# A planned attention and feed-forward kernel: 1 KB rings, a third q buffer, the sums' addition set back, the last matrix in token buffers, last units 256 and 192, two chunks not gated

## The chip, the cores and the metric

One core of one Trainium2 chip runs the whole program. The metric is the device time of one execution in microseconds; a time is the median of several runs. The engines are named as the profile names them: PE is TensorE (PEld its weight loads), DVE is VectorE, ACT is ScalarE, POOL is GpSimd, SP is SyncE, which issues all DMAs here.

## What is computed

Attention over 4 batches, 8 heads, 576 positions and 64 columns per head, in which each row keeps its 32 largest scores; then two feed-forward layers over the 2304 tokens (d_model 512). All inputs and the output are float32.

```python
scores = scale * np.matmul(q, k.transpose(0, 1, 3, 2))
kth = np.partition(scores, -top_k, axis=-1)[..., -top_k:-top_k + 1]   # top_k = 32
scores = np.where(scores >= kth, scores, -1000000000.0)
attn = np.exp(scores - np.max(scores, axis=-1, keepdims=True))
attn = attn / (np.sum(attn, axis=-1, keepdims=True) + 1e-09)
x = np.matmul(attn, v)                       # then heads side by side: 2304 x 512
h = x @ w_in;  x = np.maximum(0.01 * h, h) @ w_out            # d_ff = 2048
x = np.maximum(np.maximum(x @ w1, x @ w2), x @ w3) @ w_out2   # d_ff = 768
```

## The kernel before

**Arithmetic.** The weights arrive as pairs of 32-bit words (float64). DVE puts each 512 columns together in three passes (lines 498, 501, 504); ACT and POOL scale them and split them into two float16 parts, high and low (`split3`, lines 355 to 357). Every float32 product is three float16 matmuls (`three`, lines 874 to 876: high x high, high x low, low x high).

**Attention.** It goes in 72 steps. A step is one block of 128 tokens for one pair of heads, or a block of 64 tokens for two pairs; a batch has 18 steps. PE multiplies q and k into the one PSUM buffer `s` (line 716), ACT copies the scores to `S` (721, three buffers). DVE finds the 32 largest of each row in four MAX8 and three MATCH_REPLACE8 per half step (736, 738) and makes the mask (791, 795). ACT takes the exponential (786); ACT and POOL split it into `phl` (800, 802), and SP transposes it into `pt` by a DMA (805). PE multiplies by v into the one PSUM buffer `av` (831 to 833, the tile `sav` in the profile). DVE adds a small constant to the row sums (838) and inverts them (840), ACT scales the result into `xs` (842), ACT and POOL split it into `xhl`, and after the last pair of heads of a block SP transposes it into the token tile `xu` of its unit (868).

**Feed-forward units.** `ffn(u)` handles 192, 128, six times 256, 192 and 256 tokens. Phase H/Y makes 16 H tiles (`h_tile`, 12 matmuls each, evicted by ACT at 918 into a float tile) and adds each into four accumulators (`y_acc`). Then the result is scaled and split into `yh`, `yl` (968 to 973), with a norm over it (980). Phase M/O makes 6 tiles, each of three products joined by maximum (`m_tile`, 1011 and 1015), and adds them up (`o_acc`); ACT evicts the result (1043) and SP stores it (1053). `hilo` splits a float tile at 925 and 931. The batch's blocks finish in the order of `ORDER`; the last batch ends with two blocks of 128 and 64 tokens after 2112.

**Weights.** `prep_w` prepares w_in (kind i, 8 chunks), w_out (o, 8), w1 to w3 (t, 6) and the last matrix (z, 4). H of unit 0 waits for w_out, H of unit 1 for the last matrix, and M of unit 0 for all of t and z. The last matrix is loaded into the ring `raw`, which q, k and v of the later batches use too; its loads are put behind the loads of q and k of the second batch, and those of later batches behind it. A chunk with a gate is not loaded before a given store of the first split q or k.

**Order.** `Plan.op` registers each operation with its engine, a planned duration, what it reads and writes, and a priority. `Plan.run` (lines 125 ff.) then plays the program through with these durations: of the operations that can start at about the same time on an engine it takes the one with the lowest priority value, and an operation that needs a new buffer waits for one. The resulting order of starts is the order of each engine's queue on the chip; waits for data are made from the data flow. Tile rings have the sizes of `NB`. A ring in the set handed to `Plan` hands out buffers in any order, another in the order of the program. Second names (`hH`, `kM`, ...) limit how many buffers of a ring a phase holds: H tiles, M tiles, W for weights.

Of the kernel before, what the change touches and what calls it, by code (L numbers as in the profile page):

```python
# [27 lines left out]
PS = 2048.0  # L28
LNPS = float(np.log(PS))
P = 128  # L30
# [5 lines left out]
UN = 256  # L36
VC = 11
F0, F1, F2, F3, HB = (0, P), (P, P), (2 * P, P), (3 * P, P), (4 * P, 64)
ORDER = [[F0, HB, F1, F2, F3], [F0, F1, F2, F3, HB], [HB, F0, F1, F2, F3], [F0, F1, F2, F3, HB]]
UNITS = [192, 128] + [256] * 6 + [192, 256]  # L40

# [26 lines left out]
class Node:  # L68
    __slots__ = ("eng", "dur", "fn", "pr", "succ", "nd", "ready", "bufs", "eps", "idx", "dma")


class Plan:
# [12 lines left out]

    def op(self, eng, dur, fn, r=(), w=(), pr=0.0, dma=0.0):
        n = Node()
        n.eng, n.dur, n.fn, n.pr, n.dma = eng, dur, fn, pr, dma
        n.succ, n.ready, n.idx, n.eps = [], 0.0, len(self.nodes), self.eps
# [27 lines left out]
    eps = EPS  # L117
# [5 lines left out]
    def run(self):  # L123
# [10 lines left out]
        while len(order) < total:  # L134
# [46 lines left out]
            for m in n.succ:  # L181
                m.nd -= 1
                m.ready = max(m.ready, end + self.LAT.get((n.eng, m.eng), 0.2))
                if m.nd == 0:
                    pend[m.eng].append(m)
# [34 lines left out]
def attention_moe_kernel(ctx, tc, qk, v, w_in, w_out, w123, w2o, outT):  # L220
# [8 lines left out]

    NB = {"xu": 2, "raw": 2, "hl": 1, "k2": 7, "kt": 4, "qt": 2, "vt": 4, "S": 3, "w": 1, "m": 2, "nb": 2, "pp": 1,  # L230
          "phl": 1, "pt": 1, "r": 2, "xs": 1, "xhl": 1, "f16t": 4, "yj": 1,
          "s": 1, "av": 1, "acc": 2, "h": 4, "junk": 1, "xcap": 2, "pr": 8, "ph": 4, "ra": 3, "fi": 6, "ft": 9, "rw": 3, "fz": 3, "rc": 2, "hH": 3, "hM": 3, "hW": 1, "kH": 2, "kM": 5, "fH": 2, "fM": 2}
    PSUM_TAGS = ("s", "av", "acc", "h")
    plan = Plan(NB, {"raw", "av", "junk", "hl", "k2", "h", "f16t", "rc"})
    op = plan.op
# [16 lines left out]
    def fbuf(tag, ph, shape, dt=F32):  # L252
        b = buf(tag, shape, dt)
        b.also = (plan.buf({"h": "h", "k2": "k", "f16t": "f"}[tag] + ph, lambda: 1),)
        return b
# [103 lines left out]
    KT, QT, VT, ES = {}, {}, {}, {}  # L359
    ZL = [(("w", "z", 3), "ld")]  # L360

# [99 lines left out]

    SC = {}
    CVK = "iotz"
    CW = 512
    CVX = 0.06
    PRW0 = -13.5
    GATES = {1: [("d", 0, 0, 0, 1)], 2: [("d", 0, 1, 0, 1)]}

    def prep_w(kind, c, parts, hi, lo, colnorm, n2c, s, bi, pr, tags, guard=((), (), []), gate=()):
# [8 lines left out]
        for i, saps in enumerate(parts):  # L478
            nf = sum(n for _, n in saps)
            f = buf(tags[1], [P, 768 if tags[1] == "raw" else 512], I32)  # L480
            o = 0
            for sap, n in saps:
                raw = buf(tags[0], [P, 768])
                op(SP, 0.55, lambda raw=raw, sap=sap, n=n: Y.dma_start(raw().bitcast(I64)[:, :n], sap),
                   w=[raw, (key, "ld")] + ([(f, "ld")] if tags[1] in ("raw", "k2") or tags[0] == "raw" else []),
                   r=list(gate) + zr + (zf + [("l1", hp, a) for hp in range(HP) for a in range(2)] * (kind == "z") + guard[2] * (tags[1] == "raw") if kind in "tz" else []), pr=PRW0 if (kind, c) == ("i", 0) else pr,
                   dma=dma(P * n * 8))
# [64 lines left out]
    def wkeys(kind, cs):  # L552
        return [("W", kind, c, x, i) for c in cs for x in range(2) for i in range(WK[kind][1])]
# [6 lines left out]
    def c1(t, c):  # L560
        return t[:, c:c + 1]
# [27 lines left out]
    def w2_prep(e, pr):  # L589
        for hp in range(HP):  # L590
            if (1, hp) not in seen:
                seen.add((1, hp))
                prep_batch(1, hp)
        prep_w("z", e, [[(w2o[e, i], 384) for i in range(2)]], [w2[:, e, 0]], [w2[:, e, 1]],
               None, c1(cz, e), c1(sz, e), c1(bz, e), pr, ("raw", "fz" if e < 3 else "raw"),
               ({0: ["ZB"], 3: [("ZZ", 2)]}.get(e, []), [("ZZ", e - 1)] if e in (1, 2) else [],
                [("ZZ", e - 1)] if e else ["ZB"]))
# [79 lines left out]

    EXPP = 4
    COLD = 1.7
    NCOLD = 8  # L680
# [13 lines left out]
    def attention(i):  # L694
# [143 lines left out]
        op(DVE, 0.07, lambda: V.tensor_scalar(r()[:n, 0:nh].rearrange("p (x h) -> p x h", h=2),  # L838
                                             av()[:n, 0:nh // 2, :, 64], 1e-9 * PS, None, op0=ALU.add), r=[avb], w=[(r, 0)], pr=pr)
        op(DVE, 0.08, lambda: V.reciprocal(r()[:n, 4:4 + nh], r()[:n, 0:nh]), r=[(r, 0)], w=[(r, 1)], pr=pr)  # L840
# [45 lines left out]

    MAXP = 40
    FINP = 40
    CS = 0.8
# [3 lines left out]
    def ffn(u, pr0, between=None):  # L893
# [4 lines left out]
        t3 = 3 * mm(N)  # L898
        acc, ak, ast, a0 = accs(N)
        clock = [pr0]  # L900
# [7 lines left out]
        def h_tile(f):  # L908
            pr = tick(1.3)
            c = f // (FCI // P)  # L910
            p = fbuf("h", "H", [P, 512])
            wk = wkeys("i", [c]) + wkeys("o", range(8)) * (u == 0) + wkeys("z", range(4)) * (u == 1)
            for k in range(KC):
                op(PE, t3, lambda k=k: three(p()[:, :N], lambda x: wi[:, x, k, f * P:(f + 1) * P],
                                             lambda x: xu()[:, x, k, :N], k == 0, k == KC - 1),
                   r=xk + wk, w=[p], pr=pr)
            rr = fbuf("k2", "H", [P, 2, UN])
            op(ACT, act(N, True, 1), lambda: A.activation(rr()[:, 0, :N], p()[:, :N], AF.Prelu,  # L918
# [81 lines left out]
        def m_tile(f):  # L1000
            t = fbuf("k2", "M", [P, 2, UN])
            wk = wkeys("t", [f]) + (wkeys("t", range(NF2)) + wkeys("z", range(4))) * (u == 0)
# [185 lines left out]
```

## Time and profile before

| | |
|---|---|
| median of 3 runs | 1149.49 us (1147.88 to 1154.09) |
| profiled execution | 1152.11 us |
| its span, first to last instruction | 1150.2 us |
| PE / PE weight loads busy | 912.4 / 797.7 us |
| DVE busy | 973.6 us |
| ACT / POOL busy | 757.3 / 680.6 us |
| DMA moved | 125.79 MB, 44.6% of 16 engines' span |

The profile comes from one execution. An engine is busy while one of its instructions runs; what it waited for before an instruction is read from the semaphore that came last. L838 is line 838 of the kernel. A row of waits gives who waited, for whom, total us, times, and the longest. In the timeline a merged row gives its start, its length, engine, line, operation, tiles written and read, shapes and count.

### The profile page before, as it was taken

Reading aid. Unit: us, or ns where it says so; the run is one execution under the profiler, and the core shown is the slowest. Engines: PE = TensorE matmul, PEld = TensorE weight load, DVE = VectorE, ACT = ScalarE, POOL = GpSimd, SP = SyncE. Lnnn points to the kernel's source line nnn. Section 1 sums busy time; section 2 is a strip of 40 time slices with the busy share of each in tenths; the row PEclk is TensorE's granted clock in tenths of the full one; section 3 lists DMA queues with packets and bytes.
Section 4 is the critical chain, followed back from the end, with each engine's and each line's share of the span. In section 5 each row is a group of like instructions: output and inputs, shape, how many; then the busy total and the mean of one; then the engine's idle time right before and its main releaser. Section 6 shows DMA issues by size and latency. Waiting matters only on the chain.

```text
span 1150.2 us, 27408 instructions
## 1 busy us (share of the span) xinstructions
PE 912.4 (79%) x10294; PEld 797.7 (69%) x10294; DVE 973.6 (85%) x2154; ACT 757.3 (66%) x1625; POOL 680.6 (59%) x1054
## 2 busy tenths in 40 slices
PE   3253246853299799999899989989998998998998
PEld 2131235742199788887688778878887887898987
DVE  3989999989989999999899899899999999995001
ACT  7667747886457767567778665686786666665331
POOL 5555646875446766566777655575787556555231
PEclk9999998975599999999999999999999999999999
DMA  7758455654354423235574333364573433332000
GB/s 234 250 141 264 147 159 166 176 122 134 96 122 88 96 64 83 62 73 131 139 184 118 65 79 70 60 149 78 146 164 66 87 77 52 79 64 52 20 1 19
DMA packets 268549, 125.79 MB, mean 109 GB/s; under 512 B 237440, under 2 KB 255360, under 8 KB 266368
## 3 DMA queue, kind: packets, MB, share of 16 engines
q1 hardware_dynamic: 268416, 124.04, 44.6%
q8 instruction: 81, 1.33, 0.5%
q14 instruction: 52, 0.43, 0.1%
HBM read 62.65 MB, written 14.16 MB: 67 GB/s over the span
## 4 chain that ended last, share of the span: by engine, by line
PE 40%; DMA 14%; DVE 11%; POOL 7%; ACT 6%; issue 5%; SPq 1%; POOLq 0%; ACTq 0%; DVEq 0%
DMA pt<-phl 12%; PE h L874 7%; PE h L875 7%; PE h L876 7%; PE acc L875 4%; DVE m L736 4%; PE acc L874 4%; PE acc L876 4%; DVE w L738 3%; PE sav L716 3%; POOL phl L802 3%; PE sav L831 2%; PE sav L832 2%; PE sav L833 2%; POOL f16t L931 1%
## 5 line engine op out<-in xcount | busy, mean ns | idle before, releaser
L736 DVE MAX8 m<-w 128x8 f32<-128x576 f32 x432 | 309.7, 746 | 0.1
L931 POOL TENSOR_TENSOR f16t<-k,f16t 128x256 f16<-128x256 f32 (+2 forms) x220 | 142.8, 651 | 195.1 <-ACT f16t L925 184.1
L738 DVE MATCH_REPLACE8 w<-m,w 128x576 f32<-128x576 f32 x288 | 211.9, 741 | 0.0
L802 POOL TENSOR_TENSOR phl<-pp,phl 128x576 f16<-128x576 f32 x144 | 183.7, 1281 | 45.5 <-ACT phl L800 43.9
L874 PE MATMUL h<-k,w 128*128 128x256 f16 (+2 forms) x720 | 187.0, 264 | 7.8 <-ACT k L971 5.5
L875 PE MATMUL h<-k,w 128*128 128x256 f16 (+2 forms) x720 | 186.9, 264 | 3.7 <-POOL k L973 3.6
L876 PE MATMUL h<-k,w 128*128 128x256 f16 (+2 forms) x720 | 186.8, 264 | 0.0
L716 PE MATMUL sav<-kt,qt 128*128 128x288 f16 (+5 forms) x800 | 110.1, 288 | 77.1 <-ACT S L721 56.2
L875 PE MATMUL acc<-f16t,wo 128*128 128x256 f16 (+2 forms) x640 | 164.9, 262 | 4.7 <-POOL f16t L931 4.6
L874 PE MATMUL acc<-f16t,wo 128*128 128x256 f16 (+2 forms) x640 | 165.0, 262 | 0.0
L876 PE MATMUL acc<-f16t,wo 128*128 128x256 f16 (+2 forms) x640 | 165.0, 262 | 0.0
L874 PE MATMUL h<-xu,wi 128*128 128x256 f16 (+1 forms) x576 | 155.8, 270 | 5.0 <-ACT k L918 2.2
L876 PE MATMUL h<-xu,wi 128*128 128x256 f16 (+1 forms) x576 | 155.8, 271 | 0.0
L875 PE MATMUL h<-xu,wi 128*128 128x256 f16 (+1 forms) x576 | 155.8, 271 | 0.0
L800 ACT ACTIVATE phl<-pp 128x576 f16<-128x576 f32 x144 | 97.8, 681 | 65.0 <-DMA pt<-phl 27.8
L786 ACT ACTIVATE pp<-S,nb,colt 128x576 f32<-128x576 f32 x144 | 121.5, 860 | 20.6 <-POOL nb L776 12.7
L716 PEld LDWEIGHTS <-qt 128*128 128x128 f16 (+1 forms) x800 | 65.2, 109 | 99.8 <-issue 75.9
L798 POOL TENSOR_TENSOR pp<-pp,S 128x576 f32<-128x576 f32 x72 | 92.2, 1280 | 69.8 <-DVE S L795 42.9
L925 ACT ACTIVATE f16t<-k 128x256 f16<-128x256 f32 (+2 forms) x220 | 85.3, 392 | 59.9 <-DVE k L1015 57.2
L831 PE MATMUL sav<-vt,pt 128*128 128x65 f16 (+1 forms) x800 | 91.2, 202 | 38.5 <-DMA pt<-phl 34.1
L918 ACT ACTIVATE k<-h,colt 128x256 f32<-128x256 f32 (+2 forms) x160 | 71.1, 451 | 70.5 <-PE h L876 69.3
L721 ACT ACTIVATE S<-sav 128x576 f32<-128x576 f32 x144 | 92.8, 644 | 32.2 <-PE sav L716 18.4
(133 smaller groups left out, 2629.5 us busy)
## 6 DMA issues: line engine op xcount, KB each, us to landing
w<-in_w SPq DMA_DIRECT2D x18, 512.0 KB, 3.9
w<-in_w_in SPq DMA_DIRECT2D x8, 1024.0 KB, 6.6
w<-in_w_out SPq DMA_DIRECT2D x8, 1024.0 KB, 4.9
raw<-in_qk SPq DMA_DIRECT2D x24, 288.0 KB, 3.4
dqk<-hl SPq DMA_DIRECT2D x48, 144.0 KB, 2.5
kt<-dqk SPq DMA_DIRECT2D x16, 288.0 KB, 3.3
qt<-dqk SPq DMA_DIRECT2D x144, 32.0 KB, 2.2
raw<-in_v SPq DMA_DIRECT2D x12, 352.0 KB, 3.5
```

Of the source, the lines that this page charges most:

```text
L716: T.matmul(p()[osl, h, o:o + w], q()[:, hh, st, :n], k()[:, hh, kc:kc + w], start=st == 0, stop=st == 1, skip_group_check=True)
L721: op(ACT, act(S, True), lambda t=t, p=p: A.activation(t().rearrange("p (a s) -> p a s", a=2), p()[:, :, :288], AF.Copy), r=[p], w=[(Sp, j) ...
L736: op(DVE, dve(S) * 1.03, lambda mc=mc, src=src: V.max(mc(), src()), r=rd, w=[(m, j, 0, r)], pr=pd)
L738: op(DVE, dve(S) * 1.03 + 0.06, lambda mc=mc, src=src, j=j: V.match_replace(out=wj(j), in_to_replace=mc(), in_values=src(), imm_value=NEG) ...
L786: op(ACT, act(S, aps=2), lambda j=j, es=es: A.activation(pp()[:, j], Sb[j](), AF.Exp, bias=nb()[:, j:j + 1], scale=es[:, 0:1]), r=[(Sp, j) ...
L800: op(ACT, act(S), lambda j=j: A.activation(phl()[:, 0, j], pp()[:, j], AF.Copy), r=[(pp, j)], w=[(phl, 0, j)], pr=pr)
L802: op(POOL, pool(S), lambda j=j: G.tensor_tensor(phl()[:, 1, j], pp()[:, j], phl()[:, 0, j], op=ALU.subtract), r=[(pp, j), (phl, 0, j)], w= ...
L831: T.matmul(o, hc, vh, start=c == 0, stop=False, skip_group_check=True)
L874: T.matmul(out, wt(0), xt(0), start=first, stop=False, skip_group_check=True)
L875: T.matmul(out, wt(0), xt(1), start=False, stop=False, skip_group_check=True)
L876: T.matmul(out, wt(1), xt(0), start=False, stop=last, skip_group_check=True)
L931: op(POOL, pool(N) + 0.044, lambda: G.tensor_tensor(hl()[:, 1, :N], g()[:, 0, :N], hl()[:, 0, :N], op=ALU.subtract), r=[(g, 0), (hl, 0)], ...
```

## The change

The edits go together.

- The last two units are 256 and 192 tokens instead of 192 and 256.
- An operation can have a `lag`, by which the plan takes it to be ready later. The addition at line 838 gets 3.0 us.
- The float tiles of H and M (256 columns of 4 bytes) move from the ring `k2` (2 KB, 7 buffers, now 5) to a ring `k1` (1 KB, 3 buffers, at most 2 for H and 2 for M). H may hold 2 PSUM buffers instead of 3.
- q has 3 buffers instead of 2.
- The last matrix is loaded into buffers of the ring `xu` (two, handed out in order) instead of `raw`; its fourth piece is put together there too. Its loads no longer wait for the second batch's loads, and later loads of q, k and v no longer wait for it (`ZL`).
- The second chunk of w_in has no gate; the third chunk and the matrices t are gated by an earlier store than before.
- The planned duration of the conversion passes through PSUM is 0.06 us shorter (`CVX`).

`G1 = 4` and an empty `PRE` come in as well; with these values they do nothing.

```diff
-UNITS = [192, 128] + [256] * 6 + [192, 256]
+UNITS = [192, 128] + [256] * 7 + [192]
...
-    def op(self, eng, dur, fn, r=(), w=(), pr=0.0, dma=0.0):
+    def op(self, eng, dur, fn, r=(), w=(), pr=0.0, dma=0.0, lag=0.0):
...
-                m.ready = max(m.ready, end + self.LAT.get((n.eng, m.eng), 0.2))
+                m.ready = max(m.ready, end + self.LAT.get((n.eng, m.eng), 0.2) + m.lag)
...
-    NB = {"xu": 2, "raw": 2, "hl": 1, "k2": 7, "kt": 4, "qt": 2, "vt": 4, ...
+    NB = {"xu": 2, "raw": 2, "hl": 1, "k2": 5, "k1": 3, "kt": 4, "qt": 3, "vt": 4, ...
...
-          ... "hH": 3, "hM": 3, "hW": 1, "kH": 2, "kM": 5, "fH": 2, "fM": 2}
+          ... "hH": 2, "hM": 3, "hW": 1, "kM": 5, "jH": 2, "jM": 2, "fH": 2, "fM": 2}
...
-    ZL = [(("w", "z", 3), "ld")]
+    ZL = []
...
+    ZT = "xu"
...
-    CVX = 0.06
+    CVX = 0.0
...
-    GATES = {1: [("d", 0, 0, 0, 1)], 2: [("d", 0, 1, 0, 1)]}
+    GATES = {1: [], 2: [("d", 0, 0, 0, 1)]}
...
     def w2_prep(e, pr):
-        for hp in range(HP):
+        for hp in range(HP) if ZT == "raw" else ():
             if (1, hp) not in seen:
                 seen.add((1, hp))
                 prep_batch(1, hp)
...
-               None, c1(cz, e), c1(sz, e), c1(bz, e), pr, ("raw", "fz" if e < 3 else "raw"),
+               None, c1(cz, e), c1(sz, e), c1(bz, e), pr, (ZT, "fz" if e < 3 else ZT),
...
+    RLAG = 3.0
...
-                                             av()[:n, 0:nh // 2, :, 64], 1e-9 * PS, None, op0=ALU.add), r=[avb], w=[(r, 0)], pr=pr)
+                                             av()[:n, 0:nh // 2, :, 64], 1e-9 * PS, None, op0=ALU.add), r=[avb], w=[(r, 0)], pr=pr, lag=RLAG)
...
-            rr = fbuf("k2", "H", [P, 2, UN])
+            rr = fbuf("k1", "H", [P, 1, UN])
...
-            t = fbuf("k2", "M", [P, 2, UN])
+            t = fbuf("k1", "M", [P, 1, UN])
```

## Rows read from the trace of the kernel before

**Rows 1.** Page, parts 1 and 2: busy time by engine; granted clock in 40 slices.

```profile
PE 912.4 (79%) x10294; PEld 797.7 (69%) x10294; DVE 973.6 (85%) x2154; ACT 757.3 (66%) x1625; POOL 680.6 (59%) x1054
...
PEclk9999998975599999999999999999999999999999
```

**Rows 2.** By stretch: length, busy us (count) of PE, PEld, DVE, ACT, POOL; clock, DMA.

```profile
10.00:26.00 16.00, 6.47 (x24) 4.85 (x25) 5.10 (x16) 14.55 (x30) 10.38 (x28) 1.00 0.74 228
250.00:317.00 67.00, 20.38 (x182) 14.86 (x182) 62.81 (x143) 38.87 (x81) 35.93 (x54) 0.50 0.44 114
325.00:1062.00 737.00, 684.75 (x8113) 608.85 (x8111) 678.83 (x1509) 501.09 (x1135) 464.72 (x703) 1.00 0.44 94
1062.00:1151.00 89.00, 82.23 (x771) 73.71 (x768) 7.95 (x19) 29.23 (x71) 21.00 (x37) 1.00 0.04 13
```

**Rows 3.** Timeline of SP, POOL, PE: last matrix, unit 0's second phase; its loads' landing.

```profile
255.11 7.55 SPq L484 DMA_DIRECT2D raw<-in_w2o  x3
...
313.78 1.65 POOL L357 TENSOR_TENSOR w<-raw,w 128x768 f16<-128x768 f32 x1 [2.12 <-ACT w L356]
...
316.82 0.35 PE L874 MATMUL h<-k,w 128*128 128x192 f16 x1
...
raw<-in_w2o SPq DMA_DIRECT2D x8, 384.0 KB, 3.3
```

**Rows 4.** Waits of PE, 325 to 1062 us: total, times, longest.

```profile
PE sav L831 <- DMA pt<-phl: 18.8, 23, 1.6
PE sav L716 <- ACT S L721: 11.2, 16, 1.6
```

**Rows 5.** Waits of DVE, 100 to 1062 us.

```profile
DVE r L838 <- PE sav L833: 40.7, 37, 2.8
...
DVE r L838 <- PE sav L716: 5.3, 4, 2.3
...
DVE r L838 <- ACT S L721: 2.1, 2, 1.1
```

**Rows 6.** Timeline of DVE: two MAX8, and two additions in a row.

```profile
442.79 1.41 DVE L736 MAX8 m<-w 128x8 f32<-128x576 f32 x2
447.61 0.15 DVE L838 TENSOR_SCALAR r<-sav 128x2 f32<-128x2 f32 x1
...
461.14 0.15 DVE L838 TENSOR_SCALAR r<-sav 128x2 f32<-128x2 f32 x1
```

**Rows 7.** Waits of DVE, 0 to 317 us.

```profile
DVE r L838 <- PE sav L833: 6.2, 6, 2.2
...
DVE r L838 <- PE sav L716: 4.2, 2, 2.2
```

**Rows 8.** Second chunk of w_in: load, first pass, a pass's time, landing time.

```profile
34.83 1.41 SPq L484 DMA_DIRECT2D w<-in_w_in  x3
...
57.97 1.27 DVE L498 TENSOR_SCALAR acc<-w 128x512 int32<-128x512 int32 x2
...
L498 DVE TENSOR_SCALAR acc<-w 128x512 int32<-128x512 int32 x32 | 20.6, 683 | 1.8 <-DMA w<-in_w_in 1.8
...
w<-in_w_in SPq DMA_DIRECT2D x8, 1024.0 KB, 6.6
```

**Rows 9.** Last unit: transposed tokens, first and last matmuls, landing of such transposes.

```profile
1063.63 1.19 SPq L868 DMA_TRANSPOSE xu<-xhl  x1
...
1069.97 0.27 PE L874 MATMUL h<-xu,wi 128*128 128x256 f16 x1
...
1145.84 0.27 PE L876 MATMUL acc<-f16t,w 128*128 128x256 f16 x1
...
xu<-xhl SPq DMA_TRANSPOSE x20, 2.8
```

**Rows 10.** Waits of ACT on the transposing DMA; the H tiles' evictions.

```profile
ACT phl L800 <- DMA pt<-phl: 27.8, 20, 4.5
...
L918 ACT ACTIVATE k<-h,colt 128x256 f32<-128x256 f32 (+2 forms) x160 | 71.1, 451 | 70.5 <-PE h L876 69.3 <-POOL f16t L931 0.6
```

More of the change, by code (lines that the diff above doesn't have):

```diff
@@ L68 @@
 class Node:
-    __slots__ = ("eng", "dur", "fn", "pr", "succ", "nd", "ready", "bufs", "eps", "idx", "dma")
+    __slots__ = ("eng", "dur", "fn", "pr", "succ", "nd", "ready", "bufs", "eps", "idx", "dma", "lag")
 class Plan:
@@ L84, in buf @@
         return b
-    def op(self, eng, dur, fn, r=(), w=(), pr=0.0, dma=0.0):
+    def op(self, eng, dur, fn, r=(), w=(), pr=0.0, dma=0.0, lag=0.0):
         n = Node()
-        n.eng, n.dur, n.fn, n.pr, n.dma = eng, dur, fn, pr, dma
+        n.eng, n.dur, n.fn, n.pr, n.dma, n.lag = eng, dur, fn, pr, dma, lag
         n.succ, n.ready, n.idx, n.eps = [], 0.0, len(self.nodes), self.eps
@@ L228, in attention_moe_kernel @@
     ctx.enter_context(tc.manual_schedule())
-    NB = {"xu": 2, "raw": 2, "hl": 1, "k2": 7, "kt": 4, "qt": 2, "vt": 4, "S": 3, "w": 1, "m": 2, "nb": 2, "pp": 1,
+    NB = {"xu": 2, "raw": 2, "hl": 1, "k2": 5, "k1": 3, "kt": 4, "qt": 3, "vt": 4, "S": 3, "w": 1, "m": 2, "nb": 2, "pp": 1,
           "phl": 1, "pt": 1, "r": 2, "xs": 1, "xhl": 1, "f16t": 4, "yj": 1,
-          "s": 1, "av": 1, "acc": 2, "h": 4, "junk": 1, "xcap": 2, "pr": 8, "ph": 4, "ra": 3, "fi": 6, "ft": 9, "rw": 3, "fz": 3, "rc": 2, "hH": 3, "hM": 3, "hW": 1, "kH": 2, "kM": 5, "fH": 2, "fM": 2}
+          "s": 1, "av": 1, "acc": 2, "h": 4, "junk": 1, "xcap": 2, "pr": 8, "ph": 4, "ra": 3, "fi": 6, "ft": 9, "rw": 3, "fz": 3, "rc": 2, "hH": 2, "hM": 3, "hW": 1, "kM": 5, "jH": 2, "jM": 2, "fH": 2, "fM": 2}
     PSUM_TAGS = ("s", "av", "acc", "h")
-    plan = Plan(NB, {"raw", "av", "junk", "hl", "k2", "h", "f16t", "rc"})
+    plan = Plan(NB, {"raw", "av", "junk", "hl", "k2", "k1", "h", "f16t", "rc"})
     op = plan.op
@@ L253, in fbuf @@
         b = buf(tag, shape, dt)
-        b.also = (plan.buf({"h": "h", "k2": "k", "f16t": "f"}[tag] + ph, lambda: 1),)
+        b.also = (plan.buf({"h": "h", "k2": "k", "k1": "j", "f16t": "f"}[tag] + ph, lambda: 1),)
         return b
@@ L479, in prep_w @@
             nf = sum(n for _, n in saps)
-            f = buf(tags[1], [P, 768 if tags[1] == "raw" else 512], I32)
+            f = buf(tags[1], [P, 768 if tags[1] in ("raw", "xu") else 512], I32)
             o = 0
@@ L484, in prep_w @@
                 op(SP, 0.55, lambda raw=raw, sap=sap, n=n: Y.dma_start(raw().bitcast(I64)[:, :n], sap),
-                   w=[raw, (key, "ld")] + ([(f, "ld")] if tags[1] in ("raw", "k2") or tags[0] == "raw" else []),
-                   r=list(gate) + zr + (zf + [("l1", hp, a) for hp in range(HP) for a in range(2)] * (kind == "z") + guard[2] * (tags[1] == "raw") if kind in "tz" else []), pr=PRW0 if (kind, c) == ("i", 0) else pr,
+                   w=([(f, "ld")] if tags[1] in ("raw", "xu", "k2") or tags[0] in ("raw", "xu") else []) + [raw, (key, "ld")],
+                   r=list(gate) + zr + (zf + [("l1", hp, a) for hp in range(HP) for a in range(2)] * (kind == "z" and ZT == "raw") + guard[2] * (tags[1] in ("raw", "xu")) if kind in "tz" else []), pr=PRW0 if (kind, c) == ("i", 0) else pr,
                    dma=dma(P * n * 8))
@@ L887, in attention_moe_kernel @@
     MAXP = 40
+    G1 = 4
+    PRE = {}
     FINP = 40
@@ L898, in ffn @@
         t3 = 3 * mm(N)
-        acc, ak, ast, a0 = accs(N)
+        acc, ak, ast, a0 = PRE.pop(u, None) or accs(N)
+        if u == 0 and G1 == 0:
+            PRE[1] = accs(UNITS[1])
         clock = [pr0]
@@ L911, in h_tile @@
             p = fbuf("h", "H", [P, 512])
-            wk = wkeys("i", [c]) + wkeys("o", range(8)) * (u == 0) + wkeys("z", range(4)) * (u == 1)
+            wk = wkeys("i", [c]) + wkeys("o", range(8)) * (u == 0) + wkeys("z", range(G1)) * (u == 1)
             for k in range(KC):
```

## Prediction

> **What bounds the kernel now.** I read the busy shares first: VectorE (DVE) 973.6 us and TensorE (PE) 912.4 us of a span of 1150.2 us [rows 1]. A mean over the span hides three stages, so I read the busy times by stretch next [rows 2]. From 325 to 1062 us PE is busy 684.75 and DVE 678.83 of 737 us: idle 52.3 and 58.2 us, two engines that are both nearly full and wait for each other. From 1062 us PE works alone (82.2 of 89 us) on what is left of the feed-forward units. From 250 to 317 us PE does 20.4 us of work in 67 us, at a granted clock of 0.50 (the level of 1.2 GHz), while DVE is busy 62.8: DVE converts weights there, and the second phase of unit 0 waits for all of them. Its first matmul starts at 316.82 us, 1.4 us after POOL's last split of the last matrix ends (313.78 + 1.65) [rows 3].
>
> So the time is: the start of that phase, plus PE's work behind it, plus PE's idle time behind it, plus the stores. PE's idle time behind it is what can still be had: 52.3 us until 1062. The waits name it [rows 4]: 18.8 us before the attention-times-V matmuls, for the transposing DMA `pt<-phl`; 11.2 us before QK, for ScalarE (ACT) emptying the one score buffer. On DVE, 48.1 us between 100 and 1062 us are spent in front of line 838, the addition on the sums of the softmax, mostly until PE's last AV matmul (40.7 us in 37 waits) [rows 5]. This is DVE's main gap: its queue is in order, the addition was put where the plan thought AV done, and AV comes later.
>
> **The change part by part.** *The addition set back (lag 3.0).* No instruction and no run-time wait is added; in the plan the addition becomes ready 3 us after AV, so some four MAX8 or MATCH_REPLACE8 of the next step go ahead of it on DVE (each takes a slot of about 0.7 us: two MAX8 are 1.41 us in all [rows 6]). The longest of the 37 waits is 2.8 us, so 3 us covers them where other work is at hand. Behind the addition stand the reciprocal, then ACT's scaling, and the release of the single AV buffer; the next step's addition comes 13.5 us later (447.61, 461.14 [rows 6]), so the later release costs nothing unless two steps come within 3 us. What goes: 10.4 us of these waits lie before 317 us [rows 7]; I take 8 of them (ends 0 and 10.4). Behind 317 some 42 us are left (48.1 less the 6.2 of rows 7 from PE's line 833, near enough those from 100 us on). If three quarters go, DVE's idle time there falls by 31 of 58, somewhat over half.
>
> But PE decides that stretch. Of its 52.3 us, 18.8 + 11.2 = 30.0 hang on attention's chain, and DVE feeds this chain. The other 22 are mostly waits within the feed-forward units, which nothing here touches. If the 30 shrink a little more than DVE's do, since the masks reach the transposes sooner as well, 20 us go (ends 0 and 30). Why not 31, as on DVE: PE is next in line, with 52 us of slack at most, and its order is fixed by the same plan.
>
> *Two chunks not gated.* The second chunk of w_in is issued at 34.83 us and converted from 57.97 us on. Without the gate its load can go with the first loads, and its six DVE passes (3 lines x 2, 0.68 us each: 4.1 us [rows 8]) fit between 10 and 26 us, where DVE is busy 5.1 of 16 us [rows 2]. Gain up to 4.1 us, as DVE bounds the stage up to 317. Against it: such a load takes 6.6 us to land [rows 8], and if it stands ahead of the stores and loads of the first q and k, the first step starts up to 6.6 us later. Ends -4.1 and +6.6; I take -2, because DMA is busy 0.74 between 10 and 26 us [rows 2] and has room. The Trainium skill, "DMA: Bandwidth & Descriptors", section "Queues, rings and completion order", says that on one DMA engine the descriptors of a queue are consumed in ring order, which speaks against this edit: by it the +6.6 end would hold in full and the sum below would be 8.6 us longer (a rival below). No row here shows that order by itself.
>
> *The last matrix in token buffers.* The eight loads (384 KB, 3.3 us each to land) begin at 255.11 us and the last split begins at 313.78 [rows 3]. They no longer share two buffers with the second batch's q and k, nor wait for its loads. But the first of them must still wait for the third matrix, whose raw buffers lie in the same memory as its results; the last piece still needs two buffers at once. I take 0. Ends: -15 us (eight loads one after another are 26.4 us, the stretch is 58.7; I allow half of the difference), and +8 if the tokens of unit 2, which come behind the matrix in the same ring, hold up SyncE's queue and the transposes behind it.
>
> *Last units 256 and 192.* The last unit takes 1069.97 to 1146.1 us now: 76 us for 192 + 192 + 216 + 72 = 672 matmuls, 0.113 us each, gaps included [rows 9]. With 192 columns in place of 256 I take three quarters of it, 57 us: 19 us less. These 64 tokens go into the unit before, which PE must finish first. The last tokens are transposed from 1063.63 us on (2.8 us to land [rows 9]), PE starts on them at 1069.97 and had work until then, so its total is what counts: 0 now. Only if attention became the later of the two would up to 19 us come free; with attention some 30 to 40 us earlier it is not. Ends -19 and 0.
>
> *1 KB rings, two H buffers, third q buffer, planned conversions shorter by 0.06 us.* They change buffers and planned order, not work. A unit's second phase keeps two float tiles of 256 instead of up to three; one is filled in three groups of 12 matmuls (3.9 us) and needed 2 us more, so two cover it. H matmuls have two PSUM buffers instead of three: ACT empties one in 0.45 us [rows 10], while PE does three other groups of 12. The third q buffer removes waits that DVE does not feel. 0 for all, and +28 as the bad end (below).
>
> **The sum.** Span 1150.2 - 8 - 2 (before 317) - 20 (after) = 1120.2 us; the profiled execution took 1152.11, 1.9 more than its span, so 1122.1; the median of the runs is 1149.49, a factor 0.9977: **1120 us**. Next in line is PE, with some 32 us of idle time left.
>
> **The rivals.** *The wait moves to PE:* DVE no longer stops, but AV still waits for its transposes and the units behind stay where they are. For it: 18.8 us of PE's waits name the DMA, not DVE. Only the 10 us before 317 come: 1140.2, thus 1140 us.
> *The load goes first:* +6.6 instead of -2 at the start, the rest as in the sum: 1150.2 + 6.6 - 8 - 20 = 1128.8, thus 1128 us. For it: the load is issued before the first stores. Against it: DMA has room [rows 2]. It is the case of the ring order named above.
> *All of it comes:* the matrix is ready 15 us sooner as well, and the 30 us go: 1150.2 - 10 - 15 - 30 = 1095.2, thus 1095 us. Against it: PE would run at 97% for 800 us.
> *The change doesn't do what it says:* the gap at line 838 is not a matter of order but of the one AV buffer and the one `pt`; the addition goes later in the queue and finds AV later too. 1148 us. The Trainium skill, "Perfetto Trace Analysis", section "Identifying Performance Opportunities", says of a gap that repeats on the engine that should be full that it can mean too few buffers. By that rule the edit that counts here brings nothing. Here the 37 waits name PE's matmul [rows 5], not a buffer, which speaks against it.
> *Slower:* two PSUM buffers for H. ACT stands 20 times, 27.8 us in all and up to 4.5 us, in front of line 800 until a transposing DMA has freed its buffer [rows 10]. Two buffers cover 3 x 12 x 0.11 - 0.45 = 3.5 us of that, and with FFN tiles in flight less; a third covered 1.3 us more. If ACT's waits grow past it, as a faster DVE pushes ACT to that point sooner, PE stops each time: 1150.2 - 10 + 27.8 = 1168, thus 1167 us. Against it: PE shows no wait for line 918 worth a row now.
>
> **How the numbers follow.** Forecast 0.40; load goes first 0.05; wait moves to PE 0.18; all of it 0.13; not what it says 0.11; slower 0.13. A measurement can tell about 0.5% (5.7 us) from no change. Faster: 0.40 + 0.05 + 0.13 + 0.15 of the 0.18 = 0.73. Same: 0.11 + 0.03 = 0.14. Slower 0.13. The range goes from 1086 (below the rival in which all comes, for part of the 19 us of the last unit) to 1152 (no effect, and some of the bad ends at the start); it leaves out the slower case and little of the others.
>
> **What would show it.** DVE's idle time in front of line 838 should fall from 48.1 us (from 100 us on) to under 20; the second phase of unit 0 should start near 307 us; PE's idle time from there to the end of attention should be near 32 us; the second chunk's conversion should stand before 26 us; the last H phase should start right behind the unit before it, with no gap on PE. I am wrong if PE waits for line 918 or for `pt` more than now, if the matrix comes later than 317 us, or if the waits at line 838 are as long as before.

## The result, and the profile after

The changed kernel takes 1139.24 us, the median of 6 runs (1137.15 to 1143.11), beside 1151.07 us for the kernel before on the same chip: 11.8 us less. The ratio of the two sets of runs is 0.9908 with a 95% interval of 0.9881 to 0.9935, so it is faster by 0.9%; I had forecast 29.5 us less. The profiled execution took 1139.40 us, its span is 1137.5.

The page, parts 1 and 2, against [rows 1]:

```profile
PE 920.2 (81%) x10292; PEld 804.5 (71%) x10292; DVE 978.1 (86%) x2154; ACT 759.3 (67%) x1625; POOL 679.3 (60%) x1054
...
PEclk9999987785799999999999999999999999999999
```

PE is busy 7.8 us longer than before with two matmuls fewer. Busy time by stretch, with the columns of [rows 2]:

```profile
10.00:26.00 16.00, 6.42 (x22) 4.34 (x23) 7.51 (x20) 14.86 (x29) 9.32 (x28) 1.00 0.88 277
305.00:1055.00 750.00, 697.35 (x8076) 613.99 (x8075) 688.92 (x1525) 508.30 (x1135) 469.71 (x705) 0.99 0.43 93
1055.00:1138.00 83.00, 76.75 (x863) 73.92 (x861) 9.58 (x25) 28.30 (x76) 19.36 (x39) 1.00 0.05 14
297.00:1134.00 837.00, 780.90 (x8992) 694.17 (x8989) 706.50 (x1566) 540.64 (x1220) 494.94 (x750) 0.99 0.39 84
```

The long stretch still holds two engines that are both nearly full: PE is idle 52.7 of 750 us there, DVE 61.1. In [rows 2] it was 52.3 and 58.2 of 737. The last row runs from the first matmul of unit 0's second phase, which I call M0, to the last matmul. The same stretch of the kernel before is:

```profile
317.00:1146.00 829.00, 774.86 (x8955) 690.32 (x8952) 692.26 (x1541) 534.96 (x1217) 489.48 (x745) 1.00 0.40 85
```

From M0's start, PE's busy and idle time behind it and the stores (4 us in both) the whole span follows. With the exact ends (316.82 to 1146.1 and 297.00 to 1133.5):

| | before | after | difference |
|---|---|---|---|
| start of M0 | 316.82 | 297.00 | -19.8 |
| PE busy behind it | 775.2 | 780.9 | +5.7 |
| PE idle behind it | 54.1 | 55.6 | +1.5 |
| sum | 1146.1 | 1133.5 | -12.6 |

So all of the gain lies in front of M0. Behind it, where I had put 20 us, nothing came; 7.2 us were lost.

**Where M0 starts.** PE's and POOL's timeline of the changed kernel around M0 (start, length, engine, line, operation, tiles, shapes):

```profile
296.94 0.24 PE L835 MATMUL sav<-vt,pt 128*128 128x65 f16 x1
297.00 0.35 PE L876 MATMUL h<-k,w 128*128 128x192 f16 x1
...
297.94 1.64 POOL L357 TENSOR_TENSOR w<-xu,w 128x768 f16<-128x768 f32 x1 [0.83 <-ACT w L356]
```

M0 starts right behind an AV matmul, with no wait of its own, and 0.9 us *ahead* of the last split of the last matrix. In the kernel before it also stands right behind an AV matmul, 1.4 us after the end of that split [rows 3]. So on the chip M0 does not wait for the split; its place in PE's queue decides. But this place comes from the plan, and the plan lets M0 become ready only behind all of the last matrix (`m_tile` names it among what unit 0 reads). So the two still go together: in all twenty kernels of this document M0 starts without a wait, at most 3.8 us ahead of the end of the last split and at most 1.4 us behind it. To see where M0 stands among the steps I counted the AV matmuls ahead of it. Busy time by stretch of one AV line alone, a third of all AV matmuls, in the kernel before and then in the changed one:

```profile
0.00:316.82 316.82, 25.13 (x160) 0.87 0.60 172
```

```profile
0.00:297.00 297.00, 24.18 (x150) 0.86 0.67 185
```

Ten matmuls on that line are one step of attention, twenty a step of 64 tokens, of which two stand here: M0 stands behind 14 steps before (12 x 10 + 2 x 20), behind 13 after. What one step is worth there, the additions of the kernel before show:

```profile
303.68 0.16 DVE L838 TENSOR_SCALAR r<-sav 128x2 f32<-128x2 f32 x1 [0.52 <-PE sav L833]
...
317.12 0.16 DVE L838 TENSOR_SCALAR r<-sav 128x2 f32<-128x2 f32 x1 [0.83 <-PE sav L833]
```

That is 13.4 us. The rest of the 19.8, 6.4 us, is the lag: the waits in front of the addition up to M0 fall from 10.4 us [rows 7] to 2.9. Two runs below bear this out: the lag alone on the old kernel brings M0 from 316.82 to 310.57 (-6.3, still behind 14 steps), and without it the changed kernel's M0 goes from 297.00 to 303.65 (+6.7, still behind 13), 13.2 us sooner than in the kernel before. The count of steps is no rule beyond these four: without the lag and with the old `CVX` M0 stands behind 12 steps and yet starts at 305.18.

**Why PE is busy longer behind M0.** 34 more matmuls start there (8988 against 8954; the rows above also count those that run on at their edges), 30 of them AV's of the step that moved behind it; at 774.86 / 8955 = 0.087 us each they are some 3 us. The clock may be the rest. In the changed kernel four stretches of 10 us behind M0 have a granted clock of 0.78 to 0.86, in the kernel before two; summed over all such stretches, busy time times what the clock lacks to 1 is 6.1 and 3.5 us, an estimate of 2.6 more. The two parts would make up the 5.7, but this is not shown: the kernel without the lag (below) has the same 8988 matmuls behind M0 and 6.4 us by the clock, and PE is busy only 776.3 us there. One of the four stretches, PE alone in steps of 2 us (busy, clock, DMA share, GB/s):

```profile
360.00:362.00 2.00, 0.73 (x12) 1.00 1.23 193
362.00:364.00 2.00, 1.45 (x14) 0.70 1.17 252
364.00:366.00 2.00, 2.00 (x36) 0.50 0.09 35
```

PE was idle for over half of 360 to 362, and the clock fell to 0.50, the level of 1.2 GHz, just behind. Here a wait of PE cost more than its own length.

**Where the lag's waits went.** DVE's waits between 100 and 1055 us (who waits for whom: total, times, longest), against [rows 5]:

```profile
DVE r L840 <- ACT S L723: 13.3, 14, 2.7
DVE k L1021 <- PE h L878: 11.9, 17, 1.8
DVE colt L329 <- PE acc L986: 9.0, 5, 3.9
DVE r L840 <- PE sav L718: 7.5, 10, 1.9
DVE pp L793 <- ACT pp L788: 6.4, 5, 2.6
```

The wait of the addition (now line 840) for AV, 40.7 us before [rows 5], is gone. In its place the addition waits for ACT's copy of the *next scores* and for QK, which it does not need, and DVE stops more at other places. Over the whole run its waits in front of the addition fall from 52.9 to 25.6 us, but its idle time does not fall. From M0 to the last addition, before and then after, with the columns of [rows 2]:

```profile
316.82:1060.73 743.91, 691.66 (x8175) 615.51 (x8173) 683.99 (x1521) 506.18 (x1146) 468.48 (x708) 1.00 0.44 94
```

```profile
297.00:1057.29 760.29, 706.44 (x8152) 622.29 (x8150) 697.81 (x1543) 512.71 (x1144) 475.58 (x711) 0.99 0.43 91
```

DVE is idle 59.9 us there before and 62.5 after. On PE, from M0 to 1055 us, against [rows 4]:

```profile
PE sav L833 <- DMA pt<-phl: 16.7, 18, 2.2
PE h L876 <- ACT k L977: 5.2, 5, 1.6
PE sav L718 <- ACT S L723: 5.0, 7, 1.8
PE h L876 <- ACT k L1017: 4.5, 3, 2.2
PE sav L718 <- DVE r L840: 4.0, 6, 1.5
```

The last row is new: QK waits for the addition. One such place in the changed kernel's timeline:

```profile
736.42 0.19 PE L835 MATMUL sav<-vt,pt 128*128 128x65 f16 x1
...
738.74 0.66 PE L718 MATMUL sav<-kt,qt 128*128 128x64 f16 x6
...
736.00 1.41 DVE L738 MAX8 m<-w 128x8 f32<-128x576 f32 x2
740.12 0.16 DVE L840 TENSOR_SCALAR r<-sav 128x2 f32<-128x2 f32 x1 [2.71 <-ACT S L723]
...
739.44 0.65 ACT L723 ACTIVATE S<-sav 128x576 f32<-128x576 f32 x1 [0.68 <-PE sav L718]
```

AV was done at 736.6 and DVE was free at 737.4. But the next QK (738.74) and the copy of its scores (739.44) stood ahead of the addition in the plan's order, and the addition waited for both, 2.71 us. The reason is in the tile: `sav` spans two PSUM banks, the scores `s` are its columns 0 to 287 and `av` its columns 288 to 417 of the same banks. The program makes engines that touch these banks follow each other in the plan's order. An addition that the plan sets back 3 us falls behind such a copy more often: by the starts in the traces, in the 72 steps no copy stands between AV and the addition 69 times before, 34 times after (one 25 times, two 13 times), and 63 times in the changed kernel without its lag. The Trainium skill, "PSUM — Partial Sum Buffer", section "PSUM bank collisions raise a hardware error", says that the compiler back end's scheduler adds a dependency between any two instructions on different engines that touch the same bank in the same 32 partitions, reads and writes alike, and that a different address there still collides. The 2.71 us above agree with the added dependency; the collision itself no run here shows.

The kernel before had such waits too. [rows 5] has 7.4 us of the addition behind QK and the score copy, neither of which makes what it reads, and from 317 to 1061 us QK waited for the scaling of AV:

```profile
PE sav L716 <- ACT xs L842: 1.6, 4, 0.6
```

**The other places.** Second chunk's first pass, first MAX8, first and last matmul of the last unit, in the changed kernel's timeline:

```profile
18.58 1.29 DVE L499 TENSOR_SCALAR acc<-w 128x512 int32<-128x512 int32 x2
...
27.88 0.76 DVE L738 MAX8 m<-S 128x8 f32<-128x576 f32 x1 [4.52 <-ACT S L723]
...
1074.08 0.24 PE L876 MATMUL h<-xu,wi 128*128 128x192 f16 x1
...
1133.22 0.25 PE L878 MATMUL acc<-f16t,w 128*128 128x192 f16 x1
```

The second chunk is converted before 26 us, as forecast; the first step starts 1.7 us later than before (26.17 us there). The last unit takes 59.4 us, and starts 4 us later than in [rows 9].

### The profile page after: what moved, and what is told of

The parts are those of the page before. It is cut to its first block, busy times and chain, and to the rows that moved or that the text cites. A ratio compares the mean times of both kernels' runs of the same rounds, so it can differ in the third digit from the quotient of the medians.

```text
span 1137.5 us, 27381 instructions
## 1 busy us (share of the span) xinstructions
PE 920.2 (81%) x10292; PEld 804.5 (71%) x10292; DVE 978.1 (86%) x2154; ACT 759.3 (67%) x1625; POOL 679.3 (60%) x1054
## 4 chain that ended last, share of the span: by engine, by line
PE 43%; DVE 12%; DMA 10%; ACT 6%; POOL 5%; issue 4%; SPq 1%; POOLq 0%; ACTq 0%; DVEq 0%
PE h L876 7%; PE h L877 7%; PE h L878 7%; DMA pt<-phl 7%; PE acc L877 5%; PE acc L878 5%; PE acc L876 5%; DVE m L738 4%; DVE w L740 4%; PE sav L718 4%; PE sav L833 2%; PE sav L834 1%; ACT S L723 1%; POOL phl L804 1%; PE sav L835 1%
## 5 line engine op out<-in xcount | busy, mean ns | idle before, releaser
L876 PE MATMUL h<-k,w 128*128 128x256 f16 (+2 forms) x720 | 187.9, 265 | 10.6 <-ACT k L977 6.1
L877 PE MATMUL acc<-f16t,wo 128*128 128x256 f16 (+2 forms) x640 | 167.8, 266 | 7.5 <-POOL f16t L937 7.3
L876 PE MATMUL acc<-f16t,wo 128*128 128x256 f16 (+2 forms) x640 | 167.7, 266 | 0.7 <-ACT k L974 0.4
L878 PE MATMUL acc<-f16t,wo 128*128 128x256 f16 (+2 forms) x640 | 168.0, 266 | 0.0
```

What stands on the lines that cost most here:

```text
L876: T.matmul(out, wt(0), xt(0), start=first, stop=False, skip_group_check=True)
L877: T.matmul(out, wt(0), xt(1), start=False, stop=False, skip_group_check=True)
L878: T.matmul(out, wt(1), xt(0), start=False, stop=last, skip_group_check=True)
```

## The experiments

The theories. *Lag:* setting the addition back frees DVE, and the missing 20 us were lost to other edits. *Bank:* the lag itself gives its gain back, since the addition and the scores share banks. *Order:* any edit reshuffles the plan, and what is seen is M0's place and chance. A ratio to the kernel before has an interval of about 0.0025 to either side, 3 us, so two variants under some 5 us apart are hardly told apart. None of these kernels changes what is computed. A measured time is the median of a run; the split into M0, PE busy and PE idle is from the trace of one execution, which can lie a few us from the median.

### The lag

**Lag taken out of the changed kernel.**

```diff
-    RLAG = 3.0
+    RLAG = 0.0
```

> The changed kernel with the lag of the addition at 0 instead of 3 us, all else kept. Theory 'start' (the 12.7 us of the span come from unit 0's second phase starting 19.8 us sooner, and PE's idle time behind it, 55 us, is the same with any place of the addition): time within 5 us of 1139, second phase still before 303 us, the wait in front of the addition back at 45 to 55 us. Theory 'lag' (the addition's place is worth the 27 us of waits that it took away, at least in part): 1147 us or more.

Measured: 1128.31 us, 0.9817 (0.9794 to 0.9841): 10.9 us *faster* than with it. M0 starts later, at 303.65, but PE is idle only 43.5 us behind it (55.6 with the lag) and busy 776.3 (780.9). DVE's waits from 100 to 1043 us:

```profile
DVE r L840 <- PE sav L835: 18.2, 28, 3.4
...
DVE r L840 <- PE sav L718: 6.1, 4, 2.3
DVE r L840 <- ACT S L723: 5.7, 8, 1.6
```

PE's from 304 to 1043:

```profile
PE sav L833 <- DMA pt<-phl: 10.8, 13, 2.4
PE sav L718 <- ACT S L723: 8.2, 14, 1.7
```

The addition waits more (34.0 us in the whole run, 25.6 with the lag), and still PE waits less: 10.8 us for the transposes where it was 16.7. In this kernel the lag costs 11 us.

**The lag alone on the kernel before.** The argument `lag` and the line at `m.ready` as in the change, and

```diff
-... op0=ALU.add), r=[avb], w=[(r, 0)], pr=pr)
+... op0=ALU.add), r=[avb], w=[(r, 0)], pr=pr, lag=3.0)
```

> The kernel before with the lag of 3 us alone. The shared score and AV banks (theory 'bank': the addition now stands behind the next QK and the next copy of scores, and these behind it, because the score buffer and the AV buffer lie in the same two PSUM banks): the waits until AV fall from 53 us to under 10, waits of the addition for QK and for the copy of scores rise over 15 us, PE's waits of QK for the addition appear (3 us or more), the time is not better than before: 1147 to 1162 us. Theory 'lag' (the prediction's step): 1135 us or less.

Measured: 1144.73 us, 0.994 (0.9918 to 0.9962), 7 us faster; both theories' times missed, though the greater part of the waits that *Bank* named came (16.2 us of the addition for the score copy and QK, none for AV). M0 at 310.57 gives 6.3 of it; PE idle falls from 54.1 to 48.8 and PE busy rises from 775.2 to 780.1, which cancel. The addition's waits fall to 20.5 us in all. So on this base the gain before M0 is near the 8 us that I predicted, and nothing comes behind it.

**The plan's tie width moved a little,** with and without the lag: the second has `RLAG = 0.0` as well.

```diff
-EPS = 0.03
+EPS = 0.031
```

> The changed kernel with the plan's tie tolerance at 0.031 instead of 0.030 us, which changes only the order within the plan. It shows how far a plan with the same edits scatters. If the 10 us of the run without the lag are the lag's own, this one lies within 5 us of 1139; if a reshuffled plan alone gives such steps, it lies 7 us or more away.

> The same reshuffling without the lag. If the lag costs 10 us: within 5 us of 1128, and at least 6 us under the reshuffled kernel with the lag. If it was chance: at or above that one.

Measured: 1139.88 and 1126.97 us, 0.6 above and 1.3 below their counterparts. But the edit moved very little: with the lag, the queues of PE, DVE and SP are the same instruction for instruction and five places on ACT and POOL differ; without it 13 places differ in all. So these two runs are more a repeat than a reshuffle. The lag's cost comes again (-10.9, -12.9), and the theory *Order* is not tested by them.

### The shared banks

To give AV a bank of its own one has to come from the ring `h`. So the first kernel has three `h` buffers and leaves that bank empty, the second has the same order of instructions and puts AV there.

**Three h buffers.**

```diff
-... "h": 4, ... "hM": 3, ...
+... "h": 3, ... "hM": 2, ...
```

> The changed kernel with three PSUM buffers for the matmul tiles h instead of four (at most 2 for phase M), one PSUM bank left empty. It is the control of the next run. Fewer buffers cost PE some waits: 1140 to 1165 us. The addition still waits for QK and score copies 15 us or more, QK for the addition 3 us or more.

**The same, AV in its own bank.**

```diff
-    ZONE["av"] = [sav[:, :, 288:418]]
+    avt = ps.tile([P, 512], F32, name="avt")
+    ZONE["av"] = [avt[:, :260].rearrange("p (x e) -> p x e", x=2)]
```

> The same order of instructions, instruction for instruction, but the AV result has the freed PSUM bank for itself and no longer shares the banks of the scores. Theory 'bank': the addition's waits for QK and for the score copy go (under 3 us), QK's waits for the addition and for the scaling go (under 1 us), 8 us or more faster than the control. Rival 'order' (the waits stand for something else in the queues, and the lag costs because everything behind AV comes 3 us later): within 4 us of the control.

Measured: 1156.79 (1.0056, 1.0032 to 1.008) and 1140.34 us (0.9924, 0.9896 to 0.9952). Every engine's queue holds the same instructions in the same order in both, so AV's place alone is 16.5 us. M0 comes 2.8 us sooner, PE is busy 8.1 less (3.4 of it by the clock, summed as above; the rest is not explained) and idle 7.6 less. DVE's waits of the shared one, 100 to 1055 us:

```profile
DVE r L840 <- PE sav L718: 9.9, 11, 1.9
...
DVE r L840 <- ACT S L723: 6.8, 8, 1.9
DVE r L840 <- PE sav L835: 3.9, 1, 3.9
```

PE's, 300 to 1055:

```profile
PE sav L833 <- DMA pt<-phl: 17.3, 12, 6.5
...
PE sav L718 <- ACT xs L844: 4.1, 9, 0.9
PE sav L718 <- DVE r L840: 3.6, 4, 1.8
```

With AV in its own bank the addition waits for AV alone:

```profile
DVE r L841 <- PE avt L836: 14.9, 4, 8.6
```

and on PE no QK waits for the addition or the scaling any more:

```profile
PE avt L834 <- DMA pt<-phl: 22.7, 15, 6.4
PE sav L719 <- ACT S L724: 11.6, 13, 2.8
```

**Both with nearly no lag.** With a lag of 0 the plan for three h buffers finds no order, so 0.1 us stands for it. Each is the kernel above with

```diff
-    RLAG = 3.0
+    RLAG = 0.1
```

> Three h buffers, shared banks, lag 0.1 us instead of 3. If the lag costs as it does with four buffers: 7 us or more faster than the run with three buffers and lag 3.

> Three h buffers, AV in a bank of its own, lag 0.1 us; the order is that of the run before. Theory 'bank': here the lag is no longer a loss, so this one is not faster than the run with own bank and lag 3 by more than 3 us, and it is within 5 us of its own control, since with the short lag only 9 of 72 additions had a score copy between AV and themselves. Rival 'order': faster than the run with own bank and lag 3 by 7 us or more.

Measured: 1176.9 (1.0239) and 1158.76 us (1.0074). Two misses. I expected the shared bank to cost little where the lag is short; it costs 18.1 us. And the lag, which I expected to cost with shared banks, *gains* 20.1 us there (1176.9 to 1156.79) and 18.4 with AV in its own bank. So sharing has a price with three h buffers, some 17 us, with and without the lag, and it explains the new waits. With four h buffers no bank is free for AV, so the price there is not measured. Nor does it by itself explain why the lag costs 11 us there. The move gives AV another tile and another bank at once; no run tells which of the two the program's order goes by.

### The other edits, each set back in the changed kernel

**The old last units.**

```diff
-UNITS = [192, 128] + [256] * 7 + [192]
+UNITS = [192, 128] + [256] * 6 + [192, 256]
```

> The changed kernel with the last units 192 and 256 again. Theory 'PE's total' (the last units only move work from behind one border to before it): within 4 us of 1139, the last unit about 76 us long and starting about 17 us sooner. Theory 'tail' (attention's end plus the last unit set the end, and the last unit is 16.7 us shorter): the end moves with the last unit, 1149 us or more.

Measured: 1143.14 us, 3.9 slower than the changed kernel, not the 1149 or more by which the last unit would set the end.

**The last matrix in `raw` again.**

```diff
-    ZL = []
+    ZL = [(("w", "z", 3), "ld")]
...
-    ZT = "xu"
+    ZT = "raw"
```

> The changed kernel with the last matrix loaded into the old buffers again, behind the second batch's loads, and later loads behind it. If the token buffers bring the early start: the second phase of unit 0 back at 310 us or later and 1148 us or more. If not (the early start was there 23 us before, with the first load of the matrix, which waits for the third matrix in both kernels): second phase before 303 us and within 5 us of 1139.

Measured: 1134.07 us, 5.2 faster. M0 starts at 298.97, 2 us later than with token buffers.

**The old gates.**

```diff
-    GATES = {1: [], 2: [("d", 0, 0, 0, 1)]}
+    GATES = {1: [("d", 0, 0, 0, 1)], 2: [("d", 0, 1, 0, 1)]}
```

> The changed kernel with the old gates. The second chunk's six passes of 0.68 us go back among the steps, the first step starts 1.7 us sooner: second phase of unit 0 about 2 to 5 us later, 1141 to 1144 us. If the gates carry the early start by the order of the third matrix (its loads are gated too): second phase at 310 us or later, 1148 us or more.

Measured: 1145.11 us, 5.9 slower, though M0 starts at 294.08: it stands behind 12 steps here (140 matmuls on the counted line). PE busy is 785.1, idle 60.1 behind it. A sooner M0 is given back behind it.

**The old rings, two q buffers, three H buffers.**

```diff
-... "k2": 5, "k1": 3, "kt": 4, "qt": 3, ...
+... "k2": 7, "kt": 4, "qt": 2, ...
...
-... "hH": 2, ...
+... "hH": 3, ...
```

and `fbuf("k2", ..., [P, 2, UN])` in both places.

> The changed kernel with the old rings: 2 KB for the float tiles (7 buffers), two q buffers, three PSUM buffers for H. The prediction put these at 0: within the scatter of 1139 (5 us). If the two H buffers cost (the slower rival): 1132 us or less, with PE's waits for evictions and POOL in the feed-forward units smaller by 5 us or more. If the third q buffer or the rings bring something: 1146 us or more.

Measured: 1143.69 us, 4.5 slower.

The differences of 3.9 to 5.9 us lie at the edge of what can be told. M0 stands at 294 to 299 us in these four kernels. No single edit brings back the old place, behind 14 steps; which of them together moved it stays open.

### The same without the lag

Each of these has `RLAG = 0.0` and one edit set back, and is compared with 1128.31 us of the lag taken out alone.

**Matrix in `raw`, old `CVX`, old units, old gates.** The first, third and fourth edits are the diffs above; the second is

```diff
-    CVX = 0.0
+    CVX = 0.06
```

> The changed kernel without the lag and with the last matrix in the old buffers, behind the second batch's loads. If the matrix buffers carry the 13 us of the earlier start that the lag does not: second phase of unit 0 at 311 us or later, 1133 us or more. If they are worth nothing, as with the lag (1134 against 1139 us): start before 306 us, 1122 to 1131 us.

> The changed kernel without the lag and with the planned conversion passes 0.06 us longer again. Without the lag the second phase of unit 0 starts at 301 to 304 us, 13 us sooner than before, and neither gates, rings, units nor matrix buffers moved it by more than 3 us. If the planned duration does it (shorter passes in the plan keep the third matrix ahead of the steps): start back at 311 us or later and 1134 us or more. If not: start before 306 us and within 4 us of 1128.

> Without the lag and with the last units 192 and 256. Theory 'PE's total': within 4 us of 1128, as the 17 us move from behind a border to before it. Theory 'tail' (without the lag attention ends 12 us sooner, so PE is the bound at the end still more): 1138 us or more would speak for the tail.

> Without the lag and with the old gates. The second chunk's passes (4.1 us) go back among the steps: 1130 to 1134 us. 1128 or less: the gates bring nothing.

Measured: 1130.56 (+2.3), 1130.27 (+2.0), 1130.82 (+2.5), 1127.34 (-1.0). None can be told from nothing. The prediction had put the matrix, the conversions and the units at 0, the gates at -2.

**Rings, q and H buffers all set back; then the third q buffer alone.** The first is the diff of the old rings above; the second:

```diff
-... "qt": 3, ...
+... "qt": 2, ...
...
-    RLAG = 3.0
+    RLAG = 0.0
```

> Without the lag and with the old rings (2 KB tiles, two q buffers, three H buffers). If these carry the part of PE's idle time that fell (54 to 43 us): idle time 50 us or more and 1135 us or more. The prediction put them at 0: within 4 us of 1128.

> Without the lag and with two q buffers, the 1 KB rings kept. Old rings and two q buffers together cost 8.4 us without the lag. If it is the third q buffer: 1134 us or more and PE's idle time 48 us or more, AV's waits for the transposing DMA 15 us or more. If it is the rings (or the third H buffer): within 3 us of 1128.

Measured: 1136.74 us (0.988, 0.9855 to 0.9906) and **1118.6 us** (1117.89 to 1123.79; 0.9713, 0.9688 to 0.9738). The 1 KB rings with two H buffers bring 18.1 us, and the third q buffer costs 9.7 (1118.6 to 1128.31). The changed kernel without its lag and its third q buffer is 2.9% faster than the kernel before and beats the changed one by 20.6 us. PE's waits from 300 to 1055 us with the old rings:

```profile
PE sav L833 <- DMA pt<-phl: 17.9, 18, 2.3
PE sav L718 <- ACT S L723: 12.2, 12, 6.0
```

(of the 12.2 us, the longest wait of 6.0 lies ahead of M0), and with 1 KB rings and two q buffers:

```profile
PE h L876 <- ACT k L977: 8.3, 6, 4.3
PE sav L718 <- ACT S L723: 6.9, 9, 2.0
PE sav L833 <- DMA pt<-phl: 6.0, 9, 1.8
```

The wait for the transposes, the largest in [rows 4], falls to a third. M0 starts 4.6 us sooner (302.17 to 297.52), and PE's idle time behind it goes from 50.1 to 40.9 us. Both hold within the profiled executions (spans 1134.8 and 1122.0); that of the faster kernel was its slowest run, so its median shows more. Why more room in the rings, but not for q, lets the transposes come sooner I could not read from the traces; it stays open.

These runs also price the lag beside each edit that is set back. The kernel with the lag is slower by 12.3 us with the old units (1143.14, 1130.82), by 17.8 with the old gates, by 7.0 with the old rings and by 3.5, too little to tell, with the matrix in `raw`. So with four h buffers the lag costs in each of these kernels, and how much depends on the other edits. Since it costs with the old rings too, these alone are not what turns its sign against the kernel before, where it gains 7 us.

The runs side by side (us):

| kernel | median | M0 | PE busy behind | PE idle behind |
|---|---|---|---|---|
| before | 1151.07 | 316.82 | 775.2 | 54.1 |
| after | 1139.24 | 297.00 | 780.9 | 55.6 |
| lag alone on before | 1144.73 | 310.57 | 780.1 | 48.8 |
| after, no lag | 1128.31 | 303.65 | 776.3 | 43.5 |
| no lag, old rings | 1136.74 | 302.17 | 778.5 | 50.1 |
| no lag, two q | 1118.60 | 297.52 | 779.5 | 40.9 |
| after, three h | 1156.79 | 317.40 | 778.9 | 54.6 |
| three h, AV's own bank | 1140.34 | 314.61 | 770.8 | 47.0 |

## Why the prediction was right or wrong

The direction was right. The time was 19 us under the measured one, and the result lies inside the range, close to the rival in which the wait moves to PE (1140 us). That closeness is luck: the sum behind it is another, with 19.8 us gained in front of M0 and 7.2 lost behind it.

- **The lag behind 317 us, 20 us of PE's idle time: wrong, and this step decided.** It did not come: PE's idle time rose by 1.5 us. The lag itself put 12.1 us on it in the changed kernel (43.5 without it, 55.6 with it); the other edits had taken 10.6 (from 54.1). I reasoned that DVE would wait less at line 838 (right: 52.9 to 25.6 us in all, though short of "under 20"), that its idle time would fall by 31 of 58 us (wrong: 59.9 and 62.5 us from M0 to the last addition) and that PE would follow. On the kernel before, the lag alone took 5.3 us from PE's idle time and gave 5.0 back in its busy time. The order of additions and score copies is also an order on two shared PSUM banks, and I had not looked at where `s` and `av` lie. My sentence that the later release of AV "costs nothing unless two steps come within 3 us" missed that the copy of the next scores, not the next AV, comes behind. The lag's effect, a cost of 11 us in the changed kernel and a gain of 20 with three h buffers, has no settled cause: the banks explain the waits that came, not the sign.
- **The lag before 317, -8 us: right, a little less.** It measured 6.3 (the lag alone) and 6.7 (taken out).
- **M0's start: right direction, too small.** "Waits for all of them" is true of the plan and not of the chip: the plan puts M0 behind the last split, and on the chip it starts where its queue has got to, 1.4 us after that split before and 2.6 us ahead of its end now. The plan put it one step of attention sooner, which is 13.4 us that no term of mine had. With the lag that made -19.8, against the -10 of the prediction.
- **PE's work behind it, +5.7 us: a missing term.** What moves in front moves something behind: the AV step now lies behind M0, some 3 us. That the clock fell in four stretches instead of two may be the rest; that is not shown.
- **The last matrix, 0 (ends -15 and +8): inside** (setting it back: -5.2 with the lag, +2.3 without). It was costed as a wait on the chip; what it sets is M0's place in the plan.
- **Last units, 0: nothing else shown.** Setting them back costs 3.9 and 2.5 us, too little to tell. The last unit took 59.4 us (I said 57), and no gap came before it that counts: PE's total decides.
- **Gates, -2 (ends -4.1 and +6.6): inside.** The chunk was converted at 18.58 us, and the first step came 1.7 us later, not 6.6; with the load issued at 6.33 us, ahead of the stores of the first q and k, the ring order that I weighed from the Trainium skill, "DMA: Bandwidth & Descriptors", section "Queues, rings and completion order", did not hold up the first step by a whole load. Undone, +5.9 with the lag and -1.0 without.
- **Rings, third q buffer, H buffers at 0: wrong both ways, hidden in a sum.** "Buffers and planned order, not work" is no reason for 0 when the order is planned with these buffers: without the lag the rings bring 18.1 us, and the third q buffer takes 9.7 back. The slower rival's own mechanism, PE stopping for ACT's eviction of H (now line 924), hardly appeared: in the whole changed kernel PE waits once for it, 2.6 us. The prediction had read that PE shows no wait for line 918 worth a row before; it was 5.1 us in five waits.
- **"The change doesn't do what it says".** I named the one AV buffer and dismissed it, since 37 waits named PE's AV matmul. The other rows that I had added to the same 48.1 us named QK and the score copy (7.4 us in six waits [rows 5]), which the addition does not read: a sign of the shared banks that I passed over. The rule of the Trainium skill that I cited there, "Perfetto Trace Analysis", section "Identifying Performance Opportunities", that a repeated gap can mean too few buffers, no run here tests: AV kept its one buffer throughout, and what brought 16.5 us, with three h buffers, was a bank of its own.

## What to carry to other kernels

Where two engines are both at over 90%, a wait taken from one can be worth nothing: follow it to the engine beside it, with every buffer and PSUM bank that they share. A wait for an instruction whose result isn't read points at such a shared place. Where an order is planned ahead, read what stands directly in front of a key instruction in its engine's queue, and what the plan makes it stand behind, before calling its start a wait for data. Give no buffer count a cost of 0: measure each alone and in pairs, since here an edit's sign depended on the others.

## What the runs showed of the hardware

- Scores and AV in different columns of the same PSUM banks, and one tile, cost 16.5 and 18.1 us of some 1150 against AV in a bank and tile of its own, in the same order of instructions, by waits between engines that shared no data.
- PE's granted clock fell to 0.50 from 364 to 366 us, after PE had been busy for only 0.73 of the 2 us from 360 on, in the middle of a full stretch. Summed over the stretches of 10 us behind M0, busy time times what the clock lacks to 1 is 6.1 us in the changed kernel and 3.5 before, by estimate.
- The transposing DMAs `pt<-phl` (72 in each kernel) land in 4.5 us in the median in the changed kernel, 4.3 before and 3.9 in the changed kernel without the lag, with the same bytes; it is not the lag alone, since with it they take 4.0 with the matrix in `raw` or the old rings. The cause is not settled.
